# Partition sums by a transposing VectorE sum and a 16-column matmul, seven half-size output products in twelve more chunks, and a new order of loads

## The chip, the core and the metric

The kernel runs on one core of a Trainium2 chip. The metric is device time in microseconds (us), from the first to the last instruction of one execution. The engines are named as in the profile: PE is TensorE (matmuls, with PEld its weight loads), DVE is VectorE, ACT is ScalarE, POOL is GpSimd, SP is SyncE. In this kernel SP and POOL mainly issue DMAs: SP stores and transposes, POOL loads.

## The reference

Two stages are computed, one after the other. The first is a cross-covariance attention over channels, for four batches of 5824 rows and 256 channels; the second is a bilinear feed-forward on every row.

```python
def _attn_ref(q, k, v, tau):                       # q, k, v: 4 x 5824 x 256
    qn = q / (np.linalg.norm(q, axis=1, keepdims=True) + 1e-06)
    kn = k / (np.linalg.norm(k, axis=1, keepdims=True) + 1e-06)
    s = kn.transpose(0, 2, 1) @ qn / tau           # 256 x 256 for each batch
    s = s - s.max(-1, keepdims=True)
    a = np.exp(s)
    a /= a.sum(-1, keepdims=True) + 1e-09
    return v @ a

def _moe_ref(x, w1, w2, w3, w_out):                # x: 23296 x 256, d_ff = 1024
    a = x @ w1
    b = x @ w2
    h = a * b @ w3
    return h @ w_out
```

The norms run over all 5824 rows of a batch, one for each channel of q and of k. Inputs and the output are float32, and tau is 1.

## The kernel before, in words

**What is folded.** No product is wider than it must be. `W = w3 @ w_out` (1024 x 256) is computed once (`w_unit`, L803). For each batch the softmax matrix is multiplied into w1 and w2 (`fold`, L386), which gives `Wf`, so that a row's two hidden vectors come straight from v: `a = v @ Wf[0]`, `b = v @ Wf[1]`. The output is `(a * b) @ W`.

**Chunks and slots.** A batch has 45 whole row tiles of 128 rows and 64 rows over. They make twelve chunks: eleven of 512 rows, and a last one of 192 columns. The 1024 hidden features are eight blocks of 128. One chunk and one block make a *slot*: `emit_ab` (L596) issues two matmuls for a and two for b (L602, 512 columns each), ScalarE copies a out of PSUM (L608), and VectorE multiplies it with b into `abh` (L619). A batch has 96 slots; four PSUM banks, `ab0` to `ab3`, take turns, so a slot's a and b use the banks of the slot two before. A slot (c, j) is block j of chunk c; its number in the batch is 8c + j.

**The output product** of a chunk comes in two forms. `emit_half` (L640, matmuls at L650) is the plain one: 32 matmuls of 256 columns in eight parts, then one copy on ScalarE and one on VectorE. `seven_products` (L497, matmuls at L515) splits `abh` and `W` in two by two and forms seven products of half the size, as Strassen and Winograd do: 7 x 8 matmuls of 128 columns. It needs four sums of parts of `abh` first (`operand`, L530; tiles S1 to S4, one buffer each), on POOL or on VectorE as `adder` says (L508); four copies (`keep`, L525) and three additions (`join`, L528) put the result together. `seven` (L475) says which chunks take this form: all but the last two in batch 3, and those in FAST0 (batch 0) or FAST (batches 1 and 2) else.

**The scores.** While batch b's chunks run, the scores of batch n = b + 1 are made in between (`score_units`, L179): for each pair of row tiles, matmuls of q against k into `G` (L199), the squares of q and of k on ScalarE (L196), and two additions on VectorE that accumulate the squares for each partition in PSUM (L211, `accs`). These units are spread evenly over the slots of SLOTS0 (batch 0) or SLOTS. When they are done, `chain` puts the steps of `soft_units` on an agenda with due times: `norms` (L268) copies the squares out of PSUM and has POOL sum them over all partitions, `k_step` (L291) and `q_norm` (L314) turn the sums into factors, `scale`, `exps`, `sums` and eight `fold`s follow. The folds use the banks `out2` and `G` and one of the four of a and b.

**What sets the order.** Nothing is scheduled automatically: the order of each engine's instructions is the order in which this program issues them. A counter, `clock`, adds up an estimate of TensorE's time, and an agenda holds steps with due times in us on that clock, counted from the batch's start. Output parts wait in a list `pend` and are issued behind the slots, at most two sizes a slot: a plain part has size 1, one of the seven products 2. Operand sums are due every two slots after a chunk's end (`due_sums`).

**Loads.** q, k and v come in six pieces each (eight row tiles a piece) from POOL's queue, converted to bf16, into 21 shared buffers (tag `big`), which also hold `abh`. `moves` (L856 to L862) lists the due times: ("qk", n, 1, 1.0) is piece 1 of q and k of batch n at 1.0. Ahead of each load POOL waits on a small copy (`gate`, L587) until VectorE has written the latest `abh`, and, if the move before was a piece of v, on another one (`hold`, L592) until that piece has been transposed. v's transposes are DMAs on SP's queue; so are the stores.

**POOL's two libraries.** POOL's sum over partitions (L272) and its plain arithmetic (L534, L537) stand in different libraries of code. `load_library` (L815) and `load_sums` (L820) are small instructions placed so that a change of library happens at a quiet point.

Of the kernel before, what the change touches and what calls it, by code (L numbers as in the profile page):

```python
# [10 lines left out]
AF = mybir.ActivationFunctionType  # L11
# [4 lines left out]
P = 128  # L16
# [10 lines left out]
def kernel(  # L27
# [69 lines left out]
    ident_b = consts.tile([P, P], BF16)  # L97
    gate_t = consts.tile([1, 1], BF16)
# [154 lines left out]
    def soft_units(n):  # L253
# [14 lines left out]
        def norms():  # L268
            a1 = work.tile([P, 2, C], F32, tag="acc1", name=f"acc1_{n}", bufs=1)
            nc.scalar.copy(a1, accs[n])  # L270
            tot = work.tile([P, 2, C], F32, tag="s", name=f"tot_{n}", bufs=1)
            nc.gpsimd.partition_all_reduce(  # L272
                tot.rearrange("p w c -> p (w c)"), a1.rearrange("p w c -> p (w c)"), P, ReduceOp.add
            )
            st["tot"] = tot

        def k_row():

            if n == 0:
                m = psum.tile([P, 512], F32, name=f"row_{n}", **bank("ab"))  # L280
                nc.tensor.matmul(m[:, :C], lhsT=ones_pp, rhs=st["ksq"], start=True, stop=True)
                src = m[:, :C]
            else:
                src = st["tot"][:, 1, :]
            st["row"] = src
            st["kr"] = work.tile([P, C], F32, tag="kr", name=f"kr_{n}", bufs=1)
            if n == 0:
                for i in range(4):
                    k_step(i)
# [20 lines left out]

        def q_sums():
            st["ss"] = diagonal(st["tot"][:, 0, :].rearrange("p (c t) -> p c t", t=P))
# [112 lines left out]
        if n == 0:  # L425
# [3 lines left out]
            [(0.0, 0.0, norms), (0.0, 5.5, k_row)]  # L429
            + [(0.0, 5.5 + 1.2 * i, lambda i=i: k_step(i)) for i in range(4)]  # L430
            + [(0.0, 6.0, q_sums), (0.0, 8.5, lambda: q_norm(st["ss"]))]
            + [(0.0, 10.3 + 1.2 * ct, lambda ct=ct: scale(ct)) for ct in range(CT)]
            + [(0.0, 11.0 + 1.2 * ct, lambda ct=ct: exps(ct)) for ct in range(CT)]
            + [(0.2, 14.6, sums)]
            + [(0.43, 15.6 + 1.1 * i, lambda i=i: fold(i)) for i in range(8)]
# [39 lines left out]
    def seven(b, c):  # L475
        return c < NCH - 2 if b == B - 1 else c in (FAST if b > 0 else FAST0)
# [20 lines left out]
    def seven_products(b, c, k1, k2):  # L497
# [10 lines left out]
        adder = nc.gpsimd if b < B - 1 and c < LAST_POOL else nc.vector  # L508
# [457 lines left out]
```

## Time and profile before

| | |
|---|---|
| median of the runs | 560.07 us (560.04 to 560.08) |
| span of the profiled execution | 559.4 us |
| granted TensorE clock | 0.999 of full speed |
| a*b on VectorE (L619), mean of one | 685 ns |
| addition of squares on VectorE (L211) | 694 ns |
| a copy on ScalarE (L608), 512 columns | 584 ns |
| operand sum on POOL (L534, L537) | 2.13 us |
| operand sum on VectorE (L534, L537) | 0.685 us |
| sum over partitions on POOL (L272), three times | 3.23 us |
| weight load (LDWEIGHTS), 128 columns | 98 ns |
| DMA engines busy, 55 to 130 us | 0.95 |

The engines run side by side, and a busy share near 100% of one of them says that the others wait for it. The duration of a matmul in the profile is longer than the distance to the next, since matmuls overlap: to see what a group of them costs, take the distance between starts. In a timeline, each line gives the start, the time from the first start to the last end, the engine, the line of the kernel, the tiles written and read, and how many instructions are merged; brackets name idle time before it and what ended it.

### The profile page before, as it was taken

How to read it: one execution, taken by the hardware profiler on the slowest of the kernel's cores; microseconds unless marked ns; L12 is line 12 of the kernel's file. 1: busy time of each engine (PE TensorE's matmuls, PEld its weight loads, DVE VectorE, ACT ScalarE, POOL GpSimd, SP SyncE). 2: the span in 40 equal slices, each digit the busy share in tenths (PEclk: the TensorE clock that was granted, in tenths of full speed). 3: DMA queues.
4: the chain of work that ended last, by engine and by line, in shares of the span. 5: the costliest groups of instructions: out<-in, count | busy, mean ns of one | idle time of the engine just before them, and what ended most of it. 6: DMA issues, size and time to landing. Idle time of an engine off the chain costs nothing.

```text
span 559.4 us, 11710 instructions
## 1 busy us (share of the span) xinstructions
PE 546.9 (98%) x4393; PEld 355.1 (63%) x4403; DVE 421.6 (75%) x757; ACT 361.6 (65%) x713; POOL 193.9 (35%) x223
## 2 busy tenths in 40 slices
PE   8799999999999999999999999999999999999997
PEld 5664576766667566666657566666656666666665
DVE  1046755899977788888877688889868688888984
ACT  1046645688776878877766777777766566665663
POOL 4260013011021688889130389899320000000000
PEclk9999999999999999999999999999999999999999
DMA  9999889979547767647576767666750145141102
GB/s 215 211 179 209 154 179 238 226 148 191 131 121 145 152 132 182 150 98 130 121 172 152 138 129 173 142 131 130 185 117 39 77 92 145 59 105 41 77 39 94
DMA packets 75114, 77.57 MB, mean 139 GB/s; under 512 B 54193, under 2 KB 58801, under 8 KB 75057
## 3 DMA queue, kind: packets, MB, share of 16 engines
q0 software_dynamic: 15760, 38.93, 39.8%
q1 hardware_dynamic: 59008, 37.23, 22.6%
q8 instruction: 34, 0.56, 0.4%
q10 hardware_dynamic: 288, 0.66, 0.4%
q14 instruction: 24, 0.19, 0.1%
HBM read 78.91 MB, written 23.86 MB: 184 GB/s over the span
## 4 chain that ended last, share of the span: by engine, by line
PE 89%; DMA 7%; POOL 2%; ACT 1%; issue 1%; DVE 1%; POOLq 0%
PE a L602 27%; PE b L602 27%; PE o L650 10%; PE prodA L515 8%; PE G L199 5%; DMA k<-in_k_dram 5%; PE prodC L515 4%; PE prodB L515 2%; DMA v<-in_v_dram 2%; PE fold L375 2%; PE o_out L681 2%; PE w L806 1%; ACT as L608 0%; POOL S L537 0%; POOL w L776 0%
## 5 line engine op out<-in xcount | busy, mean ns | idle before, releaser
L619 DVE TENSOR_TENSOR abh<-as,b 128x512 bf16<-128x512 bf16 x352 | 240.2, 685 | 87.4 <-ACT as L608 82.7
L608 ACT CAST as<-a 128x512 bf16<-128x512 f32 (+1 forms) x384 | 215.8, 562 | 110.5 <-PE a L602 78.3
L602 PE MATMUL a<-vT,Wf 128*128 128x512 bf16 x704 | 209.5, 379 | 0.4 <-ACT Wf L408 0.4
L602 PE MATMUL b<-vT,Wf 128*128 128x512 bf16 x704 | 209.4, 379 | 0.0
L602 PEld LDWEIGHTS <-Wf 128*128 128x128 bf16 x1536 | 144.0, 98 | 102.4 <-issue 0.9
L211 DVE TENSOR_TENSOR acc<-acc,sq 128x512 f32<-128x512 f32 x132 | 91.6, 694 | 3.9 <-ACT sq L196 3.0
L650 PE MATMUL o<-W_sb,abh 128*128 128x256 bf16 x512 | 73.9, 273 | 0.0
L515 PEld LDWEIGHTS <-S 128*128 128x128 bf16 x864 | 57.2, 98 | 25.4 <-POOL S L537 0.8
L650 PEld LDWEIGHTS <-abh 128*128 128x128 bf16 x512 | 49.9, 98 | 26.2
L525 ACT COPY osb<-prodA 128x256 f32<-128x256 f32 x108 | 40.2, 373 | 27.4 <-PE prodA L515 27.0
L515 PEld LDWEIGHTS <-abh 128*128 128x128 bf16 x648 | 42.9, 98 | 17.9
L199 PE MATMUL G<-k,q 128*128 128x256 bf16 x276 | 47.9, 273 | 0.0
L196 ACT ACTIVATE sq<-q 128x512 f32<-128x512 bf16 x69 | 43.7, 634 | 0.5 <-DVE acc L211 0.5
L196 ACT ACTIVATE sq<-k 128x512 f32<-128x512 bf16 x69 | 43.4, 629 | 0.0
L590 POOL COPY gate_t<-abh 1x1 bf16<-1x1 bf16 x39 | 6.9, 178 | 91.5 <-DVE abh L619 90.7
L594 POOL COPY gate_t<-vT 1x1 bf16<-1x1 bf16 x16 | 3.0, 188 | 100.7 <-DMA vT<-v 100.7
L515 PE MATMUL prodA<-comb_T,S 128*128 128x128 bf16 x432 | 32.9, 219 | 0.3 <-POOL S L537 0.3
L534 POOL TENSOR_TENSOR S<-abh,abh 128x1024 bf16<-128x1024 bf16 x14 | 29.8, 2128 | 5.4 <-DVE abh L619 5.3
L537 POOL TENSOR_TENSOR S<-S,abh 128x1024 bf16<-128x1024 bf16 x14 | 29.8, 2130 | 0.8
L537 POOL TENSOR_TENSOR S<-abh 128x1024 bf16<-128x1024 bf16 x14 | 29.9, 2137 | 0.0
L537 POOL TENSOR_TENSOR S<-abh,S 128x1024 bf16<-128x1024 bf16 x14 | 29.8, 2132 | 0.0
L199 PEld LDWEIGHTS <-q 128*128 128x128 bf16 x276 | 24.5, 98 | 4.0
(124 smaller groups left out, 462.2 us busy)
## 6 DMA issues: line engine op xcount, KB each, us to landing
out_dram<-osb SPq DMA_DIRECT2D x44, 512.0 KB, 3.0
k<-in_k_dram POOLq DMA_DIRECT2D x19, 512.0 KB, 8.3
v<-in_v_dram POOLq DMA_DIRECT2D x19, 512.0 KB, 6.0
q<-in_q_dram POOLq DMA_DIRECT2D x18, 512.0 KB, 5.7
w_wout<-in_moe_w_dram POOLq DMA_DIRECT2D x1, 2048.0 KB, 23.4
k<-in_k_dram POOLq DMA_DIRECT2D x4, 320.0 KB, 7.1
v<-in_v_dram POOLq DMA_DIRECT2D x4, 320.0 KB, 4.7
q<-in_q_dram POOLq DMA_DIRECT2D x3, 320.0 KB, 5.6
```

Source lines behind the costliest of these rows:

```text
L196: nc.scalar.activation(out=sqs[0][:, :, part, :], in_=src[:, o : o + 2, :], func=AF.Square)
L199: nc.tensor.matmul(G[:, ct, :], lhsT=qt[:, i, ct * P : (ct + 1) * P], rhs=kt[:, i, :], start=(pr == 0 and part == 0 and ct == 0), stop=(pr ...
L211: nc.vector.tensor_add(accs[n], accs[n], sqs[0][:, part - 2])
L375: nc.tensor.matmul(m, lhsT=st["e"][:, c2, c1 * P : (c1 + 1) * P], rhs=w12[:, c2, w, lo:hi], start=(c2 == 0), stop=(c2 == CT - 1),)
L515: nc.tensor.matmul(st[nm][:, i, :], lhsT=a[:, j, i * P : (i + 1) * P], rhs=w[j], start=(first and j == 0 and i == 0), stop=(j == 3), skip_ ...
L525: nc.scalar.copy(quarter(r, d), st["A"])
L534: adder.tensor_add(x, a21, a22)
L537: adder.tensor_sub(x, u, w)
L602: nc.tensor.matmul(t[:, :n], lhsT=Wf[b][:, ct, w, j * P : (j + 1) * P], rhs=rhs_of(b, c, ct), start=(ct == 0), stop=(ct == CT - 1),)
L608: nc.scalar.copy(a_sb[:, :n], tiles[0][:, :n])
L619: nc.vector.tensor_mul(ab, a_sb, tiles[1])
L650: nc.tensor.matmul(t[:, k, :], lhsT=ab2[j // 4][:, j % 4, (2 * h + k) * P : (2 * h + k + 1) * P], rhs=W_sb[:, j, :], start=(j == 0 and k = ...
```

## The change

Five things are changed together.

- The sum of squares over the partitions leaves POOL. VectorE sums each 32 x 32 block with a transpose (`red`, 128 x 16), one fp32 matmul of 16 columns with the mask `fold4` adds the four groups of 32 partitions (`totals`), four ScalarE steps on 128 x 16 make the factors of q and k at once (`norm_step`), and two small steps bring them into the layouts that are needed (`spread`, `pick`). The matmul's result lies in the bank `out2`. Batch 0's own norms (n == 0) stay as they were.
- Seven products are taken in chunks 4 to 10 of batch 0 (before: 10) and in chunks 0 to 10 of batches 1 and 2 (before: 0 to 6 and 9).
- All their operand sums up to the end of batch 2 run on POOL; batch 3 keeps VectorE. The library steps go, since one library is enough.
- The seven products of a chunk come in another order, one a slot.
- Scores of batch 1 run in slots 35 to 77 (before: 41 to 75), 32 of the 92 units by slot 46; loads and the steps of the chain have new due times.

```diff
         def norms():
-            a1 = work.tile([P, 2, C], F32, tag="acc1", name=f"acc1_{n}", bufs=1)
-            nc.scalar.copy(a1, accs[n])
-            tot = work.tile([P, 2, C], F32, tag="s", name=f"tot_{n}", bufs=1)
-            nc.gpsimd.partition_all_reduce(
-                tot.rearrange("p w c -> p (w c)"), a1.rearrange("p w c -> p (w c)"), P, ReduceOp.add
-            )
-            st["tot"] = tot
+            red = work.tile([P, 16], F32, tag="red", name=f"red_{n}", bufs=1)
+            nc.vector.tensor_reduce(
+                out=red, in_=accs[n].rearrange("p w (b j) -> p (w b) j", j=32),
+                axis=mybir.AxisListType.X, op=ALU.add, apply_transpose=True,
+            )
+            st["red"] = red
+
+        def totals():
+            st["tot"] = psum.tile([P, 512], F32, tag="out2", name=f"tot_{n}", bufs=1)
+            nc.tensor.matmul(
+                st["tot"][:, :16], lhsT=fold4.rearrange("p g j -> p (g j)"), rhs=st["red"], start=True, stop=True
+            )
+
+        def norm_step(i):
+            t = st["tot"][:, :16]
+            nc.scalar.activation(
+                out=t, in_=t, func=(AF.Ln, AF.Exp)[i % 2],
+                scale=(1.0, 0.5, 1.0, -1.0)[i], bias=eps_t if i == 2 else 0.0,
+            )
+
+        def spread():
+            st["kr"] = work.tile([P, C], F32, tag="kr", name=f"kr_{n}", bufs=1)
+            nc.vector.transpose(
+                st["kr"].rearrange("p (b j) -> p b j", j=32),
+                st["tot"][:, 8:16].unsqueeze(2).to_broadcast([P, 8, 32]),
+            )
+
+        def pick():
+            t = st["tot"]
+            q4 = t[:, 16:24].rearrange("p (c g) -> p c g", g=4)
+            nc.vector.tensor_mul(
+                q4, t[:, :8].rearrange("p (c g) -> p c g", g=4), own.unsqueeze(1).to_broadcast([P, CT, 4])
+            )
+            r = work.tile([P, CT], F32, tag="r", name=f"r_{n}", bufs=2)
+            nc.vector.reduce_sum(r, q4, axis=mybir.AxisListType.X)
+            st["r"] = r
...
         return (
-            [(0.0, 0.0, norms), (0.0, 5.5, k_row)]
-            + [(0.0, 5.5 + 1.2 * i, lambda i=i: k_step(i)) for i in range(4)]
-            + [(0.0, 6.0, q_sums), (0.0, 8.5, lambda: q_norm(st["ss"]))]
-            + [(0.0, 10.3 + 1.2 * ct, lambda ct=ct: scale(ct)) for ct in range(CT)]
-            + [(0.0, 11.0 + 1.2 * ct, lambda ct=ct: exps(ct)) for ct in range(CT)]
-            + [(0.2, 14.6, sums)]
-            + [(0.43, 15.6 + 1.1 * i, lambda i=i: fold(i)) for i in range(8)]
+            [(0.0, 0.0, norms), (0.1, 2.4, totals)]
+            + [(0.0, 3.0 + 1.2 * i, lambda i=i: norm_step(i)) for i in range(4)]
+            + [(0.0, 8, spread), (0.0, 9, pick)]
+            + [(0.0, 10 + 1.4 * ct, lambda ct=ct: scale(ct)) for ct in range(CT)]
+            + [(0.0, 11 + 1.4 * ct, lambda ct=ct: exps(ct)) for ct in range(CT)]
+            + [(0.2, 15, sums)]
+            + [(0.43, 16.5 + 1.1 * i, lambda i=i: fold(i)) for i in range(8)]
         )
...
     def seven(b, c):
-        return c < NCH - 2 if b == B - 1 else c in (FAST if b > 0 else FAST0)
+        if b == B - 1:
+            return c < NCH - 2
+        return (4 if b == 0 else 0) <= c < NCH - 1
...
-        adder = nc.gpsimd if b < B - 1 and c < LAST_POOL else nc.vector
+        adder = nc.gpsimd if b < B - 1 else nc.vector
...
         return [S(1), S(2), S(3), S(4)], [
-            [p1], [p6], [p5], [p7, then(J("C", 1, 1))], [p4], [p3, then(J("C", 0, 1))], [p2, then(J("B", 0, 0)), then(store)],
+            [p1], [p2, then(J("B", 0, 0))], [p6], [p5], [p7], [then(J("C", 1, 1))], [p4], [p3, then(J("C", 0, 1)), then(store)],
         ]
...
-                wait = 0 if b == B - 1 else i + (i == 6)
+                wait = 0 if b == B - 1 else i
...
+    one = work.tile([P, 32], F32, tag="one", name="one", bufs=1)
+    nc.vector.reduce_sum(one, ident.rearrange("p (g j) -> p j g", j=32), axis=mybir.AxisListType.X)
+    nc.vector.tensor_copy(fold4, one.unsqueeze(1).to_broadcast([P, 4, 32]))
+    nc.vector.reduce_sum(own, ident.rearrange("p (g j) -> p g j", j=32), axis=mybir.AxisListType.X)
...
-    SLOTS0, SLOTS = (41, 76), (4, 71)
-    FAST0, FAST = (10,), (0, 1, 2, 3, 4, 5, 6, 9)
-    LAST_POOL = 7
-    COMB, W_SLOT = 38.0, 31
-    TO_SUMS0, TO_SUMS = 131.5, 114.0
+    SLOTS0, SLOTS = (35, 78), (4, 71)
+    EARLY, EARLY_SLOT = 32, 46
+    COMB, W_SLOT = 38, 31
...
+    def share(b, x, first, last, total):
+        if b > 0:
+            return -(-total * (x - first) // (last - first))
+        if x < EARLY_SLOT:
+            return EARLY * (x - first) // (EARLY_SLOT - first)
+        return EARLY - (-(total - EARLY) * (x - EARLY_SLOT) // (last - EARLY_SLOT))
...
-            moves = [("qk", 1, 0, 29.0), ("v", 0, 3, 30.0), ("v", 0, 4, 30.5), ("qk", 1, 1, 44.0), ("qk", 1, 2, 45.0)]
-            moves += [("qk", 1, 3, 53.0), ("qk", 1, 4, 55.0), ("v", 0, 5, 61.0), ("qk", 1, 5, 73.0)]
-            moves += [("v", 1, 0, 88.0), ("v", 1, 1, 98.0), ("v", 1, 2, 120.0), ("qk", 2, 0, 130.0)]
+            moves = [("qk", 1, 0, 29.0), ("qk", 1, 1, 29.2), ("v", 0, 3, 33), ("qk", 1, 2, 49), ("qk", 1, 3, 56)]
+            moves += [("qk", 1, 4, 62), ("v", 0, 4, 68), ("qk", 1, 5, 79), ("v", 0, 5, 88)]
+            moves += [("v", 1, 0, 99), ("v", 1, 1, 110), ("qk", 2, 0, 122)]
         else:
-            moves = [("qk", n, 1, 1.0), ("v", b, 3, 8.0), ("qk", n, 2, 21.0), ("v", b, 4, 26.0), ("qk", n, 3, 38.0)]
-            moves += [("qk", n, 4, 48.0), ("v", b, 5, 56.0), ("qk", n, 5, 69.0)]
-            moves += [("v", n, 0, 76.0), ("v", n, 1, 87.0), ("v", n, 2, 99.0), ("qk", n + 1, 0, 112.0)]
+            moves = [("qk", n, 1, 1), ("v", b, 2, 7), ("qk", n, 2, 19), ("v", b, 3, 25), ("qk", n, 3, 37)]
+            moves += [("v", b, 4, 43.5), ("qk", n, 4, 55.5), ("v", b, 5, 61), ("qk", n, 5, 72.5)]
+            moves += [("v", n, 0, 85), ("v", n, 1, 98), ("qk", n + 1, 0, 111)]
```

Removed besides: `q_sums`, the branch of `k_row` for later batches, `load_library` and `load_sums` with the places where they were put.

## The prediction

> **What bounds the kernel now.** First the page: busy shares, then the chain of work that ended last by engine.
>
> ```profile
> PE 546.9 (98%) x4393; PEld 355.1 (63%) x4403; DVE 421.6 (75%) x757; ACT 361.6 (65%) x713; POOL 193.9 (35%) x223
> ...
> PE 89%; DMA 7%; POOL 2%; ACT 1%; issue 1%; DVE 1%; POOLq 0%
> ```
>
> TensorE is busy throughout and carries 89% of the chain. A modelled busy share doesn't say whether matmuls follow each other at full rate, so I read busy time by stage, then the timeline at equal points of two chunks.
>
> ```profile
> 34.00:60.00 26.00, 24.28 (x144) 12.32 (x146) 18.21 (x33) 17.27 (x32) 4.04 (x7) 1.00 1.04 180
> 60.00:170.00 110.00, 110.00 (x749) 72.65 (x747) 85.38 (x145) 74.73 (x141) 17.18 (x39) 1.00 0.83 176
> 170.00:545.00 375.00, 374.12 (x3113) 239.80 (x3118) 308.26 (x551) 261.00 (x523) 158.21 (x149) 1.00 0.52 120
> ```
>
> Columns: stretch, length, then busy us of TensorE, weight loads, VectorE, ScalarE, GpSimd, the clock, the DMA share. From 60 to 545 us TensorE misses 0.9 us of 485. What shortens its work here shortens the run; what the other engines do costs only where TensorE must wait.
>
> ```profile
> 153.28 0.60 PE L602 MATMUL a<-vT,Wf 128*128 128x512 bf16 x2
> ...
> 163.69 0.59 PE L602 MATMUL a<-vT,Wf 128*128 128x512 bf16 x2
> ...
> 507.04 0.59 PE L602 MATMUL a<-vT,Wf 128*128 128x512 bf16 x2
> ...
> 517.08 0.59 PE L602 MATMUL a<-vT,Wf 128*128 128x512 bf16 x2
> ```
>
> Each pair of lines is one chunk apart (start us first), with no score work between: with the plain output product (L650) a chunk takes 163.69 - 153.28 = 10.41 us, with seven products (L515) 517.08 - 507.04 = 10.04 us. So a chunk that changes over gives TensorE 0.37 us back. Two waits stand out:
>
> ```profile
> 253.61 0.59 PE L602 MATMUL b<-vT,Wf 128*128 128x512 bf16 x2
> 254.50 0.62 PE L515 MATMUL prodA<-comb_T,S 128*128 128x128 bf16 x8 [0.29 <-POOL S L537]
> ...
> 302.50 0.33 PE L602 MATMUL b<-vTt,Wf 128*128 128x192 bf16 x2
> 302.94 0.61 PE L515 MATMUL prodC<-W_sb,S 128*128 128x128 bf16 x8
> ```
>
> The first product starts 0.89 us after the pair of 512-column matmuls, which takes 0.44: 0.45 us lost on GpSimd's operand sum. The second loses 0.44 - 0.16 = 0.28 us on a VectorE sum, and batch 2 repeats it at 432.68. Together 1.0 us.
>
> [...]eight 256-column matmuls stand in the chain as 0.87 us, eight of 128 columns as 0.45. [...]in 200 to 266 us, with GpSimd busy 59.1 of 66, the a*b multiply has a median of 680 ns against 689 elsewhere: no contention. [...]the change keeps VectorE to blocks of 32 and leaves the rest to TensorE, and the trace of before shows no such instruction.
>
> **The change, part by part.**
> *Twelve more chunks in seven products.* Batch 0 goes from 1 to 7, batches 1 and 2 from 8 to 11 each. 12 x 0.37 = 4.4 us off TensorE (lower end: 12 x (4 x 0.87 - 7 x 0.45) = 4.0). Each adds four ScalarE copies and three VectorE joins (373 and 419 ns) for one copy each (585 and 685): +0.9 and +0.6 us a chunk, beside TensorE.
> *Operand sums on GpSimd until batch 2's end.* VectorE loses 3 x 4 x 0.685 = 8.2 us; GpSimd gains 15 x 4 x 2.13 = 128 us. A chunk's four sums cost GpSimd 8.5 us against 10.04 without and about 11.35 with score work, plus one move of loads (two gates 0.36, two issues 1.1). It ran this mixture 90% busy from 200 to 266 us with one wait. The products are also reordered: those needing sums 2, 1, 3 and 4 come 1, 1, 1 and 2 slots later, some 1.4 us each, so I take the three waits as gone: -1.0 (ends 0 and -1.0). One library load is left, ahead of the first sum (slot 40 of batch 0). A program's first load cost 0.1 us before (37.7 us); at 12.2 us sum 2 would come 19 us after slot 40's start, and the product that needs it stands at slot 49, 18 to 19 us on: 0 (ends 0 and 1).
> *The sums over partitions.* Gone are the 3.24 us all-reduce, the changes of GpSimd's library (it stands up to 12.2 us before an instruction of the other one), a 592 ns copy, the diagonal sums, and 256-wide norms at 0.42 to 0.51 us. All lay beside TensorE: 0. New on VectorE are the transposing sum (no row; 0.695, a 512-element read as in L209, to twice that), a transpose of 256 (0.42 to 0.84) and two small ones; on ScalarE four steps of 16 columns (0.2 each, as L316). Hidden likewise while TensorE needn't wait. New in TensorE's own queue are three fp32 matmuls. The nearest rows:
>
> ```profile
> 31.84 0.70 PE L281 MATMUL row<-dk,ones_pp 128*128 128x256 f32 x2
> 32.38 0.39 PE L235 MATMUL sqq<-q 128*128 128x128 bf16 x4
> ...
> 33.79 0.38 PE L343 MATMUL sum<-ones_pp,tiny 1*128 1x2 f32 x2
> 34.10 0.39 PE L223 MATMUL warm_I-489_490<-warm 128*128 128x512 bf16 x1
> ```
>
> An fp32 matmul is two passes and holds TensorE 0.31 us for 2 columns, 0.54 for 256; for 16 I take 0.33: +1.0 for three. Behind it stand all later a and b matmuls, so a late sum stops TensorE. In batches 1 and 2 a*b of slot (8,7) ends 1.94 us after its start, 0.64 into slot (9,0); the sum ends at 1.3 to 2.0; TensorE arrives at 1.31 + 0.86 = 2.2: no wait. In batch 0 the sum lies between a*b of slots 78 and 79 and ends 2.7 to 4.0 us after 78's start, where TensorE arrives at 3.9: +0.2. Ends for all three: 0.8 and 4.
> *The later chain.* It starts at slot 78 in batch 0 (before: 76), and sums and folds are due 0.4 to 0.9 us later. In the changed program's order seven of batch 0's eight fold pairs fall into its last slot: 7 x 0.43 = 3.0 us of matmuls in a row, whose evictions take 0.69 on ScalarE and 0.75 on VectorE over few PSUM banks; VectorE's four alone need 3.0. Before, they were spread. +0.7 (0 to 1.5).
> *Score work of batch 0 over 43 slots, not 35.* In slots 72 to 79 the instructions at these durations make 10.9 us on VectorE and 10.9 on TensorE; elsewhere TensorE has more. +0.3 (0 to 1.5).
> *Loads reordered.* A move holds GpSimd until the v piece moved before it is transposed, 8.8 to 13.1 us after its issue; the moves behind v are 11 to 16 us apart, so the sums behind them are held 2 us at most, inside their slack. Pieces 0 and 1 of the next q and k come together in batch 0. Those of before landed at 79.7 and 82.1 us; the first score matmul now comes at slot 34, about 83.4. The third piece of v moves into its own batch, at 7 of the 46 us that lie before its chunk. SP's stores stand behind the v transposes as before; ACT's and SP's issues don't grow. 0, apart from the slower rival.
> *Start.* Three small VectorE instructions for the masks lie in its 23.9 us idle time before L258: 0.
>
> Sum: -4.4 - 1.0 + 1.0 + 0.2 + 0.7 + 0.3 = -3.2, so 559.4 becomes 556.2. The profiled span is 0.7 us under the median of the runs, 560.07, hence **556.9**.
>
> **The rivals.**
> *Everything new is hidden*: the burst, the transposing sum and VectorE's tight stretch cost nothing: -4.4 - 1.0 + 0.9 = -4.5, 555.6. For it: two slots of slack in the a/b banks. Against it: the burst has no such slack.
> *The gain is eaten inside the queue*: the transposing sum takes some 2 us, so that each fp32 matmul waits 0.8 us more (+2.4), and the old operand waits only move (+1.0): 556.9 + 3.4 = 560.3, no change. For it: in batches 1 and 2 my arrival at 2.2 leaves the sum 0.2 to 0.9 us. Against it: nothing on VectorE that reads 512 elements takes over 0.75 us.
> *Slower: late k pieces.* In batches 1 and 2 piece 4 is asked for at 55.5 instead of 48, behind operand sum 1 of chunk 4. That sum ends about 3.5 us after slot 40's start, the gates follow, q and k are issued at 4.2 and 4.8, and k lands after 8.3 (page), at 13.1. [...]The scores of piece 4 start at slot 50, ten slots of 1.42 later: 14.2. Slack 1.1 us. If k takes 12.9 us, as its median was between 55 and 130 us with the DMA engines at 95%, TensorE stands 3.5 us in each batch; other pieces (slack over 4 us at the same sums) stay hidden: 556.9 + 7.0 = 563.9. It decides from 8.3 + 1.1 + (3.2 + 1.1)/2 = 11.6 us on. Against it: the DMA share is 0.44 to 0.75 there, and landings then were 7.2 to 9.2.
> *Seven products don't pay*: excluded by the two chunks above.
>
> **How the numbers follow.** Forecast 0.72 (its own range 555.8 to 558.2), all hidden 0.13, eaten 0.08, slower 0.07. Less than 0.2% (1.1 us) can't be told from no change. The hidden case is faster, and a quarter of the eaten one: faster 0.87, same 0.06, slower 0.07. The range 555.0 to 559.2 takes in the hidden case and the bounds of fold burst and matmul waits.
>
> **What would show it.** Right: L515's count up by 12 x 56 = 672 and L650's down by 384; chunks of 10.04 us between scores in all batches; no operand-sum wait at TensorE. Steps are wrong if the 16-column matmul starts more than 0.5 us after the product before it, if folds at batch 0's end stand over 1.5 us, or if a wait on q or k shows at L199 or L196. A time over 559.2 makes the forecast wrong.

## The result and the profile after

The changed kernel takes **557.20 us** (median of six runs, 556.49 to 559.76) against 560.15 us for the kernel before on the same chip (560.04 to 560.70): a ratio of 0.9953, with an interval of 0.9933 to 0.9973. A second set of five runs gave 557.02 against 560.41, ratio 0.9942 (0.9930 to 0.9954). The forecast was 556.9, with a range of 555.0 to 559.2.

Two executions of the changed kernel were profiled. The first is the slowest of its six runs (559.76 us, span 558.0); the second is an ordinary one (557.50 us, span 555.7). A run's time is about 1.8 us longer than its span, so times are compared here with times and spans with spans. Both profiles are needed, since they differ in one wait.

The page of the second profile, busy time and the engines of the chain that ended last:

```profile
PE 543.9 (98%) x4697; PEld 355.6 (64%) x4697; DVE 420.9 (76%) x766; ACT 365.8 (66%) x740; POOL 308.7 (56%) x276
...
PE 84%; issue 7%; DMA 6%; POOL 2%; DVE 0%; ACT 0%; POOLq 0%
```

GpSimd has gone from 193.9 to 308.7 us of work; VectorE is where it was (421.6 before): what it loses in operand sums and in copies of the plain form it gets back in joins (L553) and the transposing sums. TensorE still carries the chain. Its busy share is 98% in both kernels, so the page alone doesn't show the gain. The two later stretches of the same profile (columns as before: stretch, length, busy us of TensorE, weight loads, VectorE, ScalarE, GpSimd, clock, DMA share):

```profile
60.00:170.00 110.00, 109.05 (x901) 73.88 (x899) 88.15 (x154) 77.85 (x158) 64.39 (x64) 1.00 0.80 167
170.00:545.00 375.00, 374.87 (x3291) 241.49 (x3289) 306.08 (x550) 263.49 (x538) 226.20 (x179) 1.00 0.55 124
```

Before 170 us TensorE now misses 0.95 us, where it missed nothing; behind 170 us it misses 0.13, where it missed 0.88. What TensorE waited for, first in the second profile, then in the first (columns: us in total, times, longest):

```profile
PE G L200 <- DMA k<-in_k_dram: 0.9, 1, 0.9
```

```profile
PE prodA L540 <- POOL S L562: 1.6, 1, 1.6
PE w L837 <- DMA w3T<-w_wout: 0.6, 1, 0.6
PE G L200 <- DMA k<-in_k_dram: 0.6, 1, 0.6
```

The wait of a score matmul for piece 0 of k is in both, and the kernel before had none. The wait for an operand sum, in chunk 9 of batch 0, is in the first alone.

The work itself is as forecast. The groups of the seven products (L540) have one of 624 matmuls and five of 312, 2184 in all (before 1512: 672 more), and the plain product (L675) has 128 (before 512). One chunk without score work in batch 1, in the second profile:

```profile
279.26 0.59 PE L627 MATMUL a<-vT,Wf 128*128 128x512 bf16 x2
...
289.30 0.59 PE L627 MATMUL a<-vT,Wf 128*128 128x512 bf16 x2
```

Eight slots apart: 10.04 us, where the plain form took 10.41.

The new operations, groups of the second profile with shapes kept apart (columns: total busy us, mean ns of one, idle before):

```profile
L272 DVE TRANSPOSE_TENSOR_REDUCE red<-acc 128x16 f32<-128x512 f32 x3 | 2.1, 709 | 0.0
L286 ACT ACTIVATE tot<-tot 128x16 f32<-128x16 f32 x9 | 1.6, 182 | 0.5 <-PE tot L280 0.5
L293 DVE STREAM_TRANSPOSE kr<-tot 128x256 f32<-128x256 f32 x3 | 1.3, 444 | 0.0
```

The transposing sum takes 0.71 us, the lower end of what was allowed for it. The 16-column matmul, by the timeline of the second profile:

```profile
156.95 0.61 PE L540 MATMUL prodB<-W_sb,abh 128*128 128x128 bf16 x8
157.40 0.35 PE L280 MATMUL tot<-red,fold 128*128 128x16 f32 x2
157.59 0.59 PE L627 MATMUL a<-vT,Wf 128*128 128x512 bf16 x2
```

It starts 0.45 us after the product before it, which is that product's own length, so it waits for nothing; and the next matmul starts 0.19 us behind it (0.14 in batches 1 and 2).

**Where the time went.** The start of slot 32 of batch 0 and the start of the last slot of batch 3 lie 475.41 us apart before, 472.44 in the second profile: -2.97. The steps below add up to the same. What happens ahead of slot 32 is the start, which the change hardly touches. The profile of before held one wait of 1.0 us there (44.6 us, a transpose of v on TensorE) that the second profile doesn't have; it comes from one execution to the next and is left out of the sum.

### The profile page after: what moved, and what is told of

It is laid out like the page before. It is cut to its first block, busy times and chain, and to the rows that moved or that the text cites. A ratio compares the mean times of both kernels' runs of the same rounds, so it can differ in the third digit from the quotient of the medians.

```text
span 558.0 us, 12429 instructions
## 1 busy us (share of the span) xinstructions
PE 546.5 (98%) x4697; PEld 357.1 (64%) x4697; DVE 420.9 (75%) x766; ACT 366.3 (66%) x740; POOL 308.7 (55%) x276
## 4 chain that ended last, share of the span: by engine, by line
PE 83%; DMA 11%; POOL 4%; issue 0%; SPq 0%; DVE 0%; ACT 0%; POOLq 0%; DVEq 0%
PE a L627 25%; PE b L627 25%; PE prodA L540 12%; PE prodC L540 6%; DMA k<-in_k_dram 6%; PE G L200 5%; DMA w_wout<-in_moe_w_dram 4%; PE prodB L540 3%; PE fold L398 2%; PE o L675 2%; PE o_out L706 2%; POOL S L562 2%; DMA w3T<-w_wout 1%; PE w L837 1%; SPq L757 0%
## 5 line engine op out<-in xcount | busy, mean ns | idle before, releaser
L540 PEld LDWEIGHTS <-S 128*128 128x128 bf16 x1248 | 82.6, 98 | 36.5 <-POOL S L562 1.8
L550 ACT COPY osb<-prodA 128x256 f32<-128x256 f32 x156 | 58.1, 373 | 43.7 <-PE prodA L540 43.1
L540 PEld LDWEIGHTS <-abh 128*128 128x128 bf16 x936 | 61.9, 98 | 25.5
L559 POOL TENSOR_TENSOR S<-abh,abh 128x1024 bf16<-128x1024 bf16 x29 | 61.8, 2131 | 21.3 <-DVE abh L644 14.7
L562 POOL TENSOR_TENSOR S<-S,abh 128x1024 bf16<-128x1024 bf16 x29 | 61.7, 2127 | 1.9
L562 POOL TENSOR_TENSOR S<-abh,S 128x1024 bf16<-128x1024 bf16 x29 | 61.9, 2135 | 0.1
L562 POOL TENSOR_TENSOR S<-abh 128x1024 bf16<-128x1024 bf16 x29 | 61.8, 2132 | 0.1
L540 PE MATMUL prodA<-comb_T,S 128*128 128x128 bf16 x624 | 47.6, 219 | 1.6 <-POOL S L562 1.6
L200 PE MATMUL G<-k,q 128*128 128x256 bf16 x276 | 48.4, 273 | 0.6 <-DMA k<-in_k_dram 0.6
L553 DVE TENSOR_TENSOR osb<-prodC,osb 128x256 f32<-128x256 f32 x78 | 32.5, 417 | 0.1
L200 PEld LDWEIGHTS <-q 128*128 128x128 bf16 x276 | 23.5, 98 | 3.8 <-issue 0.7
L540 PE MATMUL prodC<-W_sb,S 128*128 128x128 bf16 x312 | 23.8, 219 | 0.1
```

The lines of the kernel that those rows point to most:

```text
L200: nc.tensor.matmul(G[:, ct, :], lhsT=qt[:, i, ct * P : (ct + 1) * P], rhs=kt[:, i, :], start=(pr == 0 and part == 0 and ct == 0), stop=(pr ...
L540: nc.tensor.matmul(st[nm][:, i, :], lhsT=a[:, j, i * P : (i + 1) * P], rhs=w[j], start=(first and j == 0 and i == 0), stop=(j == 3), skip_ ...
L550: nc.scalar.copy(quarter(r, d), st["A"])
L553: nc.vector.tensor_add(quarter(r, d), st[nm], quarter(r, d))
L559: adder.tensor_add(x, a21, a22)
L562: adder.tensor_sub(x, u, w)
```

## The experiments

Two questions had to be settled: which of the five parts of the change carry the gain, and what sets the waits that are left in batch 0. "Changed kernel" below stands for 557.02 us, ratio 0.9942. All ratios are to the kernel before, measured beside each. Its median lay between 560.27 and 560.75 us in these sets, so differences of some 0.5 us from the changed kernel say nothing.

### The changed kernel once more

> The changed kernel once more, unaltered. In its first profile TensorE stood 1.8 us at 169.5 us (a product waits for operand sum 4 of chunk 9 of batch 0), 0.7 us at 83.4 (the first score matmul waits for piece 0 of k) and 0.8 us at 68.7 (a matmul of w waits for the transposed w3). Theory: the first comes from the order of GpSimd's queue and is there again, within 0.5 us; the other two come from when a transfer lands and differ from run to run by up to 1 us each, which is why the timed runs (556.5 to 558.3) spread wider than the kernel before (560.0 to 560.7). Rival: all three are fixed parts of the new order and return within 0.2 us each. Time 556.5 to 558, ratio 0.993 to 0.997.

557.02 us, 0.9942 (0.9930 to 0.9954). The wait for k came again (1.1 us in distance of starts, 0.9 by the list above). The wait for w3 didn't, and the 1.8 us wait at 169.5 us didn't either: the theory named it as fixed and was wrong there. TensorE at slot 91 of batch 0, in the first profile and then in the second:

```profile
169.38 0.33 PE L627 MATMUL b<-vTt,Wf 128*128 128x192 bf16 x2
171.33 0.62 PE L540 MATMUL prodA<-comb_T,S 128*128 128x128 bf16 x8 [1.62 <-POOL S L562]
```

```profile
168.89 0.33 PE L627 MATMUL b<-vTt,Wf 128*128 128x192 bf16 x2
169.05 0.61 PE L540 MATMUL prodA<-comb_T,S 128*128 128x128 bf16 x8
```

The product is the one that reads sum 3 of chunk 9 (sum 3, not 4, as the expectation has it). In the second profile GpSimd makes that sum from 166.7 to 168.9 us, 0.2 us ahead of its product: there is next to no slack. In the first GpSimd had stood until 157.3 us for piece 0 of v of batch 1, transposed at 157.2, and in the second until 154.8 (transposed at 154.7). So this wait hangs on when a load lands. The changed kernel's runs spread over 3.3 us in the first set and the kernel before's over 0.7, but in the second set it is 0.8 and 1.6: that the change makes the time spread wider, as the expectation has it, isn't shown.

### The new partition sums alone

The kernel before with `norms`, `totals`, `norm_step`, `spread` and `pick` in place of the all-reduce, with their due times, and without the library steps:

```diff
-            nc.gpsimd.partition_all_reduce(...)
+            nc.vector.tensor_reduce(out=red, ..., apply_transpose=True)
...
-            if all(c >= LAST_POOL for c in FAST0):
-                at(0.0, 0.0, load_library)
```

> The kernel before, with the new partition sums alone (transposing sum, 16-column matmul, short norm steps, their due times); the chunks in seven products, who adds, product order, loads and score slots stay. Theory of the prediction (all that was removed lay beside TensorE): no gain by itself; three fp32 matmuls add 3 x 0.19 = 0.6 us, the folds' burst 0.2, the old operand waits stay: +0.5 to +1.2 us, ratio 1.001 to 1.002. Rival (taking the all-reduce and the library changes off GpSimd brings time of itself, since the first operand sums come sooner): 1 us or more faster than before, ratio under 0.998.

560.97 us, 1.0009 (1.0001 to 1.0017): 0.5 us slower, as the theory said. The old operand wait is still there (all that TensorE waited for between 60 and 545 us):

```profile
PE prodA L538 <- POOL S L560: 0.3, 1, 0.3
```

So taking 3.2 us off GpSimd three times, with its library changes, brings nothing by itself. Whether it is needed for the rest isn't shown: no run keeps the all-reduce and has all operand sums on GpSimd.

### The twelve chunks alone

The kernel before with `seven` as in the changed kernel; all-reduce, loads and product order stay, and chunks 7 to 10 have their sums on VectorE:

```diff
-        return c < NCH - 2 if b == B - 1 else c in (FAST if b > 0 else FAST0)
+        return c < NCH - 2 if b == B - 1 else (4 if b == 0 else 0) <= c < NCH - 1
```

> The kernel before, with seven products in the same twelve more chunks alone; the all-reduce stays on GpSimd, so the operand sums of chunks 7 to 10 are VectorE's. Theory (the twelve chunks pay only because GpSimd takes all the sums): in chunks 7 and 8 VectorE has some 5.5 a*b + 1.3 joins + 3.8 additions of squares + 2.7 sums = 13.3 us against some 11.4 on TensorE, about 2 us lost in each; two or three such chunks a batch cancel the 4.4 us: 559 to 564, ratio 0.998 to 1.007, with VectorE's sums named at TensorE's waits. Rival (the engine of the sums does not matter, 12 x 0.37 us arrive whole): 555.5 to 557, ratio 0.992 to 0.995.

577.81 us, 1.0320 (1.0304 to 1.0336): 17.4 us slower. The theory had the sign and not the size (559 to 564). The first operand sum on GpSimd, by its timeline:

```profile
95.67 0.53 POOL L119 DMA_DIRECT2D k<-in_k_dram  x1 [0.19 <-issue]
107.57 2.11 POOL L534 TENSOR_TENSOR S<-abh,abh 128x1024 bf16<-128x1024 bf16 x1 [11.37 <-DVE osb L658]
```

VectorE's copy named as releaser is the one that happened to end then. Behind the load the trace has two events that change GpSimd's library (MODIFY_POOL_CONFIG), at 96.3 us, and nothing until 107.57: 11.2 us for the change. TensorE stood 4.5 us for that sum. To see whether this was all, the library of the sums was loaded at the batch's start, where GpSimd has nothing to do:

```diff
+            at(0.0, 0.0, load_sums)
             at(15.0, 0.0, transpose_w3)
```

> The kernel before with seven products in twelve more chunks, as in e2_seven_only, but with GpSimd's library of sums loaded at the start of batch 0, where GpSimd has nothing to do. In e2_seven_only the first sum stood 11.2 us behind a load of that library and TensorE stood 4.5 us for it at 108.5 us; the rest of the 17.4 us was spread over chunks 7 to 10 of each batch. Theory (the rest is VectorE's: the sums of chunks 7 to 10 do not fit beside the score additions, and the second library change holds GpSimd's loads): 4 to 6 us less than e2_seven_only, 572 to 574, still ratio 1.02 or more. Rival (the library load at the start was what put all later work out of step): 557 to 562.

577.25 us, 1.0302 (1.0289 to 1.0315). The first wait went, and 0.6 us came of it. Another stood behind it; all that TensorE waited for between 60 and 545 us:

```profile
PE prodA L515 <- POOL S L537: 5.8, 2, 5.4
PE prodB L515 <- DVE osb L528: 4.0, 8, 1.7
PE prodC L515 <- DVE osb L528: 3.9, 4, 1.6
PE b L602 <- DVE abh L619: 1.4, 6, 0.5
```

One long wait for a GpSimd sum (GpSimd had stood 9.6 us, until 124.0, for the transposed last piece of v), and many for VectorE's joins, which stand behind VectorE's own operand sums. Both the expected 4 to 6 us and the rival fell; only "still 1.02 or more" held.

The list doesn't hold all that a long wait costs. The first of these two runs, behind its wait of 4.4 us, by stretches (columns as in the result, the clock third from the end):

```profile
113.00:117.00 4.00, 3.73 (x22) 2.57 (x23) 0.77 (x2) 2.01 (x4) 3.99 (x6) 0.50 1.05 206
118.00:122.00 4.00, 4.00 (x40) 2.68 (x38) 2.97 (x7) 3.26 (x8) 3.92 (x3) 1.00 0.44 92
```

The granted clock is 0.50 from 111.0 to 117.8 us, and TensorE, which works again from 113.3, gets about half as many matmuls done: some 2 us more, by estimate. In the second run the clock is 0.50 from 128.0 to 134.8 us, behind the wait of 5.4 us: by estimate, nearly 3 us more. So the second run, too, has one long wait and one stretch of slow matmuls behind it. The next three runs take the causes apart.

### The order of the loads undone

The changed kernel with the order and due times of all loads, and the score slots (41 to 75, evenly filled), of before. These are two parts of the change, undone together:

```diff
-            moves = [("qk", 1, 0, 29.0), ("qk", 1, 1, 29.2), ("v", 0, 3, 33), ("qk", 1, 2, 49), ...]
+            moves = [("qk", 1, 0, 29.0), ("v", 0, 3, 30.0), ("v", 0, 4, 30.5), ("qk", 1, 1, 44.0), ...]
-    SLOTS0, SLOTS = (35, 78), (4, 71)
+    SLOTS0, SLOTS = (41, 76), (4, 71)
```

> The changed kernel with the loads in the order and at the due times of the kernel before, and with the scores of batch 1 in slots 41 to 75 again. Prediction of before (loads reordered: 0): no wait either way; then only the 1.1 us wait for k at 83 us goes, 555.5 to 556.5, ratio 0.990 to 0.993. Rival (the new order of loads is needed: with the old one GpSimd, now carrying 128 us more of sums, stands at loads whose buffers or v transposes are not ready, and the sums behind them come late): waits for operand sums of 2 us or more at TensorE in batches 0 to 2, 559 to 566, ratio 0.998 to 1.01.

568.24 us, 1.0142 (1.0127 to 1.0156): 8.0 us slower than before, 11 slower than the changed kernel. The rival is right, and the prediction's step is wrong as a statement on this part of the change. GpSimd's timeline, then TensorE's:

```profile
113.64 2.12 POOL L562 TENSOR_TENSOR S<-S,abh 128x1024 bf16<-128x1024 bf16 x1
124.80 0.18 POOL L619 COPY gate_t<-vTt 1x1 bf16<-1x1 bf16 x1 [9.04 <-DMA vTt<-v]
...
127.52 2.15 POOL L562 TENSOR_TENSOR S<-abh 128x1024 bf16<-128x1024 bf16 x1
129.60 2.15 POOL L562 TENSOR_TENSOR S<-abh,S 128x1024 bf16<-128x1024 bf16 x1
```

```profile
124.59 0.59 PE L627 MATMUL b<-vT,Wf 128*128 128x512 bf16 x2
129.72 0.84 PE L540 MATMUL prodA<-comb_T,S 128*128 128x128 bf16 x8 [4.54 <-POOL S L562]
```

Sums 1 and 2 of a chunk are made; then a move stands in GpSimd's queue that must first see the last piece of v transposed. It holds 9.0 us, and sums 3 and 4 behind it come late. TensorE stands until sum 3 ends at 129.67. In the kernel before, batch 0 had no sums behind that hold, so that it cost nothing. Behind the wait the clock is 0.50 until 133.4 us (some 1.7 us, by estimate), and in batch 1, at 190 us, TensorE waits 1.9 us for k. A part of the 11 us is not the loads': at the end of batch 0 TensorE waits for VectorE (0.3 and 0.4 us) as it does in the last run below, where the scores end at slot 75 too and which is 1.9 us slower for that.

### The order of the products undone

The changed kernel with the seven products in their old order:

```diff
-            [p1], [p2, then(J("B", 0, 0))], [p6], [p5], [p7], [then(J("C", 1, 1))], [p4], [p3, ...],
+            [p1], [p6], [p5], [p7, then(J("C", 1, 1))], [p4], [p3, ...], [p2, ...],
-                wait = 0 if b == B - 1 else i
+                wait = 0 if b == B - 1 else i + (i == 6)
```

> The changed kernel with the seven products of a chunk in the order of the kernel before (the products that need operand sums 2, 1, 3 and 4 one, one, one and two slots sooner). Theory (the reorder is what lets TensorE take sums from GpSimd without waiting: in batch 0 GpSimd's queue runs some 9 us behind the due times, so that sum 4 ends some 20 us after its chunk where its product would stand at 14 and now stands at 17): waits for sums come back in chunks 5 to 9 of batch 0 and behind chunk 10 of each batch, 2 to 6 us in all: 559 to 563, ratio 0.998 to 1.005. Rival (having all sums on GpSimd is enough, the order is indifferent): 556.7 to 557.5.

568.13 us, 1.0134 (1.0121 to 1.0148): 11 us more than the changed kernel, where the theory had 2 to 6, and far from the rival. GpSimd, then TensorE, at the largest wait:

```profile
117.09 2.12 POOL L562 TENSOR_TENSOR S<-abh 128x1024 bf16<-128x1024 bf16 x1
125.17 0.18 POOL L619 COPY gate_t<-vT 1x1 bf16<-1x1 bf16 x1 [5.96 <-DMA vT<-v]
...
127.89 2.16 POOL L562 TENSOR_TENSOR S<-abh,S 128x1024 bf16<-128x1024 bf16 x1
```

```profile
127.55 0.60 PE L627 MATMUL b<-vT,Wf 128*128 128x512 bf16 x2
130.10 0.62 PE L540 MATMUL prodC<-W_sb,S 128*128 128x128 bf16 x8 [1.96 <-POOL S L562]
```

It is a hold of the same kind on a transposed piece of v, here between sums 3 and 4. The changed kernel has it too, 4.4 us long in both profiles (here the first), but its product of sum 4 stands two slots later and doesn't see it:

```profile
126.23 0.18 POOL L619 COPY gate_t<-vT 1x1 bf16<-1x1 bf16 x1 [4.44 <-DMA vT<-v]
```

The waits that this kernel has over the changed one lie in batch 0 from chunk 4's products on, once in the middle of batches 1 and 2, and behind chunk 10 of each batch.

### Late sums on VectorE

The changed kernel with the sums of chunks 7 to 10 of batches 1 and 2 on VectorE:

```diff
-        adder = nc.gpsimd if b < B - 1 else nc.vector
+        adder = nc.gpsimd if b == 0 or (b < B - 1 and c < 7) else nc.vector
```

> The changed kernel with the operand sums of chunks 7 to 10 of batches 1 and 2 on VectorE, where the kernel before had those that it made. Theory (VectorE has no room for them beside the score additions): in chunks 7 and 8 VectorE has 8 x 0.685 a*b, 3 x 0.42 joins, some 5.5 x 0.694 score additions and 4 x 0.685 sums = 13.3 us against 11.2 on TensorE, 4 us a batch less what the a and b banks let it fall behind: 2 to 6 us more than the changed kernel, 559 to 563, ratio 0.998 to 1.005. Rival (VectorE makes up for it in chunks 9 and 10, and only the place of the sums in the queues counts): 556.7 to 557.7.

562.51 us, 1.0030 (1.0020 to 1.0040): 5.5 us more than the changed kernel, as the theory said. Between 60 and 545 us TensorE waited, in this execution, for:

```profile
PE G L200 <- DMA k<-in_k_dram: 2.9, 1, 2.9
PE prodC L540 <- DVE osb L553: 1.5, 4, 0.6
PE b L627 <- DVE abh L644: 0.3, 2, 0.2
```

The first line is batch 0's wait for k, unusually long here and no part of the edit; the clock is 0.50 for 3.4 us behind it, and this execution is the slowest of the nine (564.76 us). The others are VectorE's: a join that stands behind operand sums keeps a bank from the next product. From slot (7,0) of batch 1 to the batch's end takes 53.8 us against 51.7 in the changed kernel, and the same in batch 2: 4.2 of the 5.5 us are seen there.

### Fewer sums on GpSimd in batch 0

```diff
-        adder = nc.gpsimd if b < B - 1 else nc.vector
+        adder = nc.vector if b == B - 1 or (b == 0 and c == 4) else nc.gpsimd
```

> The changed kernel, with the four operand sums of batch 0's first such chunk (chunk 4) on VectorE, which has about 11 us of work there against TensorE's 15.8. Theory (GpSimd's queue runs some 9 us late in batch 0 because sums and moves of loads stand behind one another in it, so that chunk 9's sums come late): the queue is 8.5 us shorter, the 1.8 us wait at 169.5 us and the 0.3 us behind it go: 2 us less than the changed kernel, ratio to before 0.990 to 0.993. Rival (the lag is made later, by holds on the v transposes, and is not a backlog): the wait stays at 1.5 us or more, the same time as the changed kernel.

557.33 us, 0.9954 (0.9941 to 0.9967): no difference from the changed kernel, so the theory of a backlog falls. Its profile has no wait at 169.5 us, but the second profile of the changed kernel has none either, so that says nothing. The load of v's piece 4 was issued at 109.6 us here, at 109.4 and 109.9 in the changed kernel's profiles: GpSimd's queue isn't carried late from chunk 4 on, it is held again at 121 to 126 us, until the piece of that load is transposed.

### The wait for k

The scores of batch 1 from slot 36 on:

```diff
-    SLOTS0, SLOTS = (35, 78), (4, 71)
+    SLOTS0, SLOTS = (36, 78), (4, 71)
```

> The changed kernel with the scores of batch 1 from slot 36 on, not 35. In all its profiles so far TensorE stands 0.7 to 1.2 us at 82 to 84 us, because piece 0 of k lands at 83.7 to 84.2 us and the first score matmul comes before slot 35, at 82.5. Theory (the earlier scores made a new wait on k, which costs 1.1 us): one slot later, about 84.3, k is there; the wait goes and 1 us is gained: about 556, ratio 0.991 to 0.993. Rival (the wait is absorbed later, since the work behind it is bound by something else in batch 0): the same time as the changed kernel, 557.0, within 0.3 us.

557.87 us, 0.9959 (0.9946 to 0.9972). No gain. The wait at 83 us is gone from the profile, and another has come:

```profile
103.92 1.04 PE L675 MATMUL o<-W_sb,abh 128*128 128x256 bf16 x8
106.12 0.60 PE L200 MATMUL G<-k,q 128*128 128x256 bf16 x4 [1.16 <-DMA k<-in_k_dram]
```

TensorE now stands for piece 2 of k, which landed at 106.08 us, as in the changed kernel (105.65), where TensorE arrives after it. So that load was asked for earlier, ahead of piece 3 of v, with the scores again from slot 36:

```diff
-            moves = [..., ("qk", 1, 1, 29.2), ("v", 0, 3, 33), ("qk", 1, 2, 49), ...]
+            moves = [..., ("qk", 1, 1, 29.2), ("qk", 1, 2, 32), ("v", 0, 3, 33), ...]
```

> The changed kernel with the scores of batch 1 from slot 36 on, as in e4_scores_36, and with piece 2 of q and k of batch 1 asked for ahead of piece 3 of v, at about 79 us, not behind its transpose at 97. In e4_scores_36 the wait for piece 0 of k at 83 us went, and TensorE stood 1.3 us at 104.7 us for piece 2, which landed at 106.1. Theory (batch 0's front is bound by when k lands; both waits are its doing): piece 2 lands at 92 to 96 us, both waits are gone, and 1.1 us is gained: 555.7 to 556.3, ratio 0.991 to 0.993. Rivals: the three pieces share the DMA engines, so that k's first piece or v's third come later and the wait moves again (557 to 558); or the piece waits in GpSimd's queue for a buffer and the sums behind it come late (over 558).

559.13 us, 0.9972 (0.9961 to 0.9983): 2 us more than the changed kernel (1.7 by the ratios). Piece 2 of k landed at 94.7 us and both waits for k are gone. What TensorE waited for instead:

```profile
PE prodA L540 <- POOL S L562: 0.8, 1, 0.8
PE prodC L540 <- POOL S L562: 0.7, 1, 0.7
```

These waits, at 130 and 169 us, are for operand sums. So in these two runs a gain on k doesn't reach the end: in batch 0 the landing of k and GpSimd's sums are about equally late, and what TensorE saves on one it stands for the other. The expected 1.1 us was wrong twice over; the first rival of the second run named the right kind of thing: v's piece 3 landed 5 us later (97.1 us against 92.1), and the wait moved, though to the sums. All this is batch 0's: batches 1 and 2 take 129.1 and 128.7 us in both profiles of the changed kernel and in these two runs.

### Loads sooner

Piece 2 of v is transposed ahead of w3, so that GpSimd's first move is free sooner:

```diff
-            at(15.0, 0.0, transpose_w3)
             at(15.0, 0.0, lambda: transpose_piece(0, 2))
+            at(15.0, 0.0, transpose_w3)
```

> The changed kernel with two steps exchanged at the start: piece 2 of v of batch 0, which landed at 47.6 us, is transposed ahead of w3 (landed at 60.2 to 60.7) on SP's queue, not behind it at 71 us. GpSimd's first move waits for that transpose; so far q and k of batch 1 were issued at 76 to 77 us and piece 0 of k landed at 84, and with the scores one slot later TensorE stood the same 1.3 us at 105 us for piece 2 of k (landed at 106.1). Theory (batch 0's front is bound by when q and k land): the first move comes at its due time, 3 to 6 us sooner, both waits go, 1 us less than the changed kernel: 555.5 to 556.3, ratio 0.990 to 0.993. Rival (the DMA engines are full there, and the transfers land no sooner, or w3 comes later): 556.7 to 557.5.

572.88 us, 1.0219 (1.0205 to 1.0233): 16 us more than the changed kernel; the rival named the cause (w3 comes later), not the size. q and k of batch 1 were issued 7 us sooner, at 69.1 us, and piece 0 of k landed at 78.8. But then they run beside the transposes of w3. SP's timeline here, then in the changed kernel:

```profile
47.18 10.81 SPq L166 DMA_TRANSPOSE vT<-v  x1
61.08 22.39 SPq L757 DMA_TRANSPOSE w3T<-w_wout  x4
```

```profile
60.18 11.00 SPq L757 DMA_TRANSPOSE w3T<-w_wout  x4
71.23 2.07 SPq L166 DMA_TRANSPOSE vT<-v  x1
```

The fourth transpose was issued at 69.34 us and landed at 87.65: 18.3 us, against 5.1 when nothing is loaded beside it. TensorE stood for it:

```profile
74.27 1.04 PE L837 MATMUL w<-w_wout,w3T 128*128 128x256 bf16 x8
87.70 1.89 PE L837 MATMUL w<-w_wout,w3T 128*128 128x256 bf16 x8 [12.39 <-DMA w3T<-w_wout]
```

Eight such matmuls take 1.89 us behind the wait and 1.04 ahead of it: the clock is 0.50 until 92.1 us, some 2 us more by estimate. The hold that looked like lost time had kept the loads off the transposes. Behind all this, from slot 32 of batch 0 to the last slot of batch 3, this run takes 471.3 us, 1.1 less than the changed kernel in its second profile, and TensorE's list has no wait for k or for an operand sum there: with the loads that far ahead of TensorE the expected 1 us is there, but it was paid for with 16.

With this, and the scores in slots 35 to 75:

> As e8_v2_first, and with the scores of batch 1 in slots 35 to 75, not 77, so that the chain to the folds begins two slots sooner and the folds of batch 1 do not all fall into the last slot of batch 0. Theory (that burst and the waits behind it cost the 0.5 us seen at 170 us): 0.3 to 0.5 us less than e8_v2_first. Rival (VectorE, with 10.9 us of work against TensorE's 10.9 in slots 72 to 79, becomes the bound when the same additions come in two slots less): 0.5 us or more over e8_v2_first.

574.77 us, 1.0255 (1.0239 to 1.0270): 1.9 us over the run above. The rival holds: two slots less for the same additions make VectorE the bound, and b's matmuls wait for a bank that its multiply frees, five times from 136 to 170 us (1.0 us in all, 0.3 the longest). The folds can't be had sooner that way.

No version here is faster than the changed kernel.

## Why the prediction was right

The sum came out within 0.3 us of both medians, its parts less well. By its own steps, in the second profile:

| step | predicted | measured |
|---|---|---|
| twelve more chunks in seven products | -4.4 | -4.4 |
| three operand waits gone | -1.0 | -0.4 |
| three 16-column matmuls | +1.0 | +0.5 |
| their wait in batch 0 | +0.2 | 0 |
| folds in batch 0's last slot | +0.7 | +0.2 |
| VectorE tight in batch 0 | +0.3 | 0 |
| loads reordered | 0 | +1.1 |
| sum | -3.2 | -3.0 |

**Twelve chunks.** 10.04 us a chunk in batch 1 as in batch 3, and counts changed by 672 and 384. Eight matmuls of 128 columns take 0.45 us between starts, 56 ns each, in all batches (the profile gives 219 ns for one of them, since they overlap).

**The operand waits.** The sign "no operand-sum wait at TensorE" did not come out. The wait of batch 1 at 253.6 us is gone. Those behind chunk 10 shrank from 0.28 to 0.16 each, and one of 0.29 us came in batch 0 (at 170.9): 1.0 became 0.6. In some executions the 1.8 us wait for a sum of chunk 9 is added, outside the bounds of this step (0 and -1.0). "Hold the sums 2 us at most, inside their slack" is what failed: the second profile has a hold of 4.4 us at 121 to 126 us, because that piece of v was transposed 16.3 us after its issue (109.4 to 125.7), not 8.8 to 13.1. The reason given for the gain was right: with the old order 11 us are lost.

**The matmuls.** An fp32 matmul of 16 columns takes 0.14 to 0.19 us between two others, not the 0.33 that was taken from two columns in an idle queue at the start. The transposing sum is early enough everywhere, at 0.71 us.

**The folds.** Fourteen of their matmuls stand in a row at the end of batch 0:

```profile
172.98 3.40 PE L398 MATMUL fold<-w,e 128*128 128x512 bf16 x14
176.21 0.59 PE L627 MATMUL a<-vT,Wf 128*128 128x512 bf16 x2
```

3.23 us for 14 matmuls. The pair of them at 171.77 us, in the slot before, takes 0.43, so seven pairs would take 3.01: 0.2 lost. The prediction saw the burst and overrated what the evictions cost.

**The loads.** The prediction's own sign of a wrong step, a wait on k at L199 (now L200), came. "The first score matmul comes at slot 34, about 83.4" compared with landings of before (79.7 and 82.1). But the move itself came later: the transpose of v's piece 2, for which it holds, ended at 75.6 to 76.0 us and not at 73.9, behind the same transposes of w3, and k landed at 83.7 to 84.2. TensorE arrives at 82.6 and 83.5. This is 1.1 us in the second profile, 0.7 in the first; the scores that were put earlier made it. This step and the operand waits cost 1.7 us more than priced, the matmuls, their wait, the folds and VectorE together 1.5 less: that the total is right to 0.2 is partly luck, by errors that cancel.

**The profiled span.** It was said to be "0.7 us under the median of the runs"; span and time differ by 1.8 us anyway, and the profiled execution of before was in truth 1.1 us slower than its runs. The forecast is unchanged by it, since -3.2 was added to a median (560.07 - 3.2 = 556.9).

**The rivals.** "All hidden" asked for no cost beside TensorE's work, 555.6; the wait for k speaks against it. "Eaten in the queue" is excluded by the 0.71 us. "Late k pieces" in batches 1 and 2 didn't come: piece 4 landed in time in every profile of the changed kernel, and no wait on k is listed behind 85 us. Its mechanism was real, but it struck in batch 0, on piece 0. (The DMA engines were 93% busy in 55 to 130 us of before, not 95%.)

**What the prediction didn't see** is how the parts hang together. Each was priced by itself, two of them at nothing. Partition sums alone: +0.5. Seven products alone: +17. All but the loads and the score slots: +8. All but the product order: +8. Together: -3.4 (or -3.0 in the first set). The loads and the product order bring no time; without them the 4.4 us of the chunks aren't to be had, because TensorE then stands for operand sums of GpSimd that are held behind a piece of v, a hold that was harmless when no sums were behind it. A part of each of these numbers is slow matmuls behind a long wait, which nothing in the prediction priced.

Open: why the second run on k is 2 us over the changed kernel. In its profiled execution the two new waits (1.8 us) exceed the one removed (1.1) by 0.7, and the start took 0.3 longer; most of its other runs are slower still, by up to 1.4, and were not traced.

## What to carry to other kernels

When work moves onto an engine that also issues loads, look at every wait in that engine's queue, and not at its busy share: a hold that cost nothing becomes a delay for whatever is now behind it. Consumers can be put later for nothing if the order allows it; here one slot for three products and two for a fourth were worth 11 us. And before a wait is removed, find what would be waited for next: of three attempts on k the first met the next transfer, the second the next sum, and the third a collision that the old hold had prevented. Last, count a long wait of TensorE at more than its length, since the matmuls behind it ran at a granted clock of 0.50 here.

## What the runs showed of the hardware

- VectorE can sum over partitions within blocks of 32: a reduce with a transpose took a 128x512 fp32 tile in PSUM to 128x16 in 0.71 us, no longer than an addition of that size (0.69). One fp32 matmul of 16 columns, 0.14 to 0.19 us between others, does the rest. The sum over all partitions on GpSimd, in the kernel before, took 3.23 us.
- Of four DMA transposes of one weight, the last took 18.3 us when five loads were issued on the other queue at about its time (69.1 to 76.0 us), and 5.1 us without; in the next run, with the same exchange, it took 17.6.
- A change of GpSimd's library stood 11.2 us before the first operand sum when the kernel also used the other library; in the changed kernel, which uses one, the first sum followed the load before it within 0.1 us.
- Long waits of TensorE were followed by slow matmuls. From 34 us to the last 6 us of the span, six of the fourteen profiles have a wait of TensorE of 2.9 us or more, one each (2.9, 4.4, 4.5, 5.4, 11.7 and 12.4 us), and each of them has one stretch at a granted clock of 0.50, which begins in that wait or within 0.8 us of its end and lasts 3.4, 6.8, 3.4, 6.8, 13.7 and 13.7 us, in this order. All other waits there are under 2.0 us long, and there is no other such stretch.
